# Moving eleven score-maximum slots of heads 1 to 3 in a fused attention and feed-forward kernel

## The chip, the cores and the metric

The kernel runs on one core of a Trainium2 chip. The metric is the device time of one execution in microseconds (us); shorter is better. The engines are called as the profile calls them: PE is TensorE (PEld its weight loads), DVE is VectorE, ACT is ScalarE, POOL is GpSimd, and SP is the engine whose queue issues nearly all DMAs.

## The reference

Attention over 4 batches x 8 heads, 768 positions, head dimension 64, in which a query sees only the keys with the same 6-bit hash; then a feed-forward layer of 512 x 2048 on the 3072 tokens.

```python
q_bits = (np.einsum('bhsd,dk->bhsk', q, proj) > 0)
k_bits = (np.einsum('bhsd,dk->bhsk', k, proj) > 0)
q_bucket = np.sum(q_bits * powers, axis=-1)
k_bucket = np.sum(k_bits * powers, axis=-1)
mask = q_bucket[:, :, :, None] == k_bucket[:, :, None, :]
scores = scale * np.matmul(q, k.transpose(0, 1, 3, 2))
scores = np.where(mask, scores, -1000000000.0)
scores = scores - np.max(scores, axis=-1, keepdims=True)
attn = np.exp(scores)
attn = attn / (np.sum(attn, axis=-1, keepdims=True) + 1e-09)
x = np.matmul(attn, v)
...
h = x @ w_in
g = np.where(h >= 1, h, np.where(h <= -1, 0.0, (h + 1) ** 2 / 4))
out = g @ w_out
```

## The kernel before

The 32 heads go in 16 pairs. A head is worked in 12 steps (NU): two halves (`hf`) of 384 query positions by six blocks (`j`) of 128 keys. One step of the loop over `g` holds three kinds of work.

**Scores and exponentials** (`s_unit`, L372 and L373). Two matmuls put a 128x384 block of scores into one of four `s` buffers of PSUM. The second one reads rows of `T2` that hold more than the query: rows 0 to 6 hold the hash bits, so that pairs with different hashes come out very negative, and row 7 (row 32 for heads 0 and 1) holds minus the row's maximum, so the subtraction of the maximum is part of the matmul. ACT then takes the exponential twice, once rounded (`ph`, L381) and once in full (L386), and the difference of the two becomes `pl` (`lo_unit`, L39): on DVE for four of the six key blocks, on POOL for two, one step later.

**Values** (`pv_unit`, L405, L407, L409). Three matmuls of the step four earlier (LAG) accumulate the output in one of two banks, `obank` (`o0`, `o1`). Ahead of the second and of the third one, the function `between` can insert something else.

**Maxima of a later head** (`max_mm`, L311, and `max_red`, L315). The row maxima must be there before a head's scores are. For each of its six query blocks a pair of matmuls writes 128x768 scores into the tile `smax`, of which there is only one, and DVE reduces them to one column of `nm`. Where the pairs stand is a table, `early`: slot 5g+2 lies in step g behind the scores and the subtraction, 5g+3 and 5g+4 ahead of the second and third value matmul, 5g+5 at the step's end. For 5g+2 to 5g+4 `max_red` is recorded right behind its pair. For 5g+5 it is held back and recorded in the next step behind the scores, so behind everything that the step's list of tasks has put on DVE's queue.

The program has a manual schedule: each engine's queue holds its instructions in the order in which the code records them, and waits only at its head.

**Tasks around the change.** The dictionary `tasks` gives each step things to do at its end. Those that matter:

- The hash bits of pair 1 (heads 2 and 3): in steps 8 and 10 `bits_mm` (four matmuls, L211, into an `obank`, and an ACT copy `neg`, L217); in steps 9 and 11 `bits_cmp` (DVE, L222); in step 11 `bits_scale` on ACT (L272, tile `bits`); in step 12 `bits_put`, four DMAs on SP (L283) into rows 0 to 7 of `T2`. The second DMA completes what head 2's maxima read.
- The same for pair 2 (heads 4 and 5) in steps 20, 21, 23 and 24: the second `bits_cmp` and `bits_scale` are tasks of step 24, and `bits_put` one of step 25.
- The maxima of head 2 go into row 7 in two halves: `half_clamp` (DVE) in steps 18 and 23, `half_put` in steps 19 and 25: a transpose on PE (L334), an ACT copy `te` (L336), and a DMA on SP (L338). For later heads it is `max_clamp`, `max_tr` (L350) and `max_put` (L357).
- SP's queue between: `bits_put`, moves of 384 KB between partitions (`move`, L164), the load of the values (`load_v`, L287, cast on ACT in L290), the stores of finished heads, then `half_put`.

Head 2's scores begin with step 24, head 3's with step 36. From slot 155 on, in step 30, the table is filled by another rule, with heads 4 to 31.

Of the kernel before, what the change touches and what calls it, by code (L numbers as in the profile page):

```python
# [25 lines left out]
NJ = S // P  # L26
# [88 lines left out]
def attention(ctx, tc, wst, T1, T2, qk, v, pj, cv, x_d, s_d, e_d, tasks, shared):  # L115
# [490 lines left out]
    NG = NH * NU  # L606
    red = None
    early = {}
    for hd, gs in ((0, (0, 2)), (1, (4, 5, 6, 8, 11, 12)), (2, (15, 16, 17, 19, 20, 22)), (3, (21, 23, 24, 26, 27, 29))):
        early.update({5 * n + 5: (hd, NJ - len(gs) + i) for i, n in enumerate(gs)})  # L610
    for i in range(2 * NJ):
        n = 5 * 31 + 35 * i // 4
        early[n + (n % 5 == 1)] = 4 + i // NJ, i % NJ
# [494 lines left out]
def lsh_attn_ffn(ctx: ExitStack, tc: tile.TileContext, qk, v, pj, cv, w_in, w_out, out):  # L1108
# [101 lines left out]
    for i in (2, 3):  # L1210
        at(NH * NU + 2 * i - 10, late[i + NFT - NW1][0])
    attention(actx, tc, wst, T1, T2, qk, v, pj, cv, x_d, s_d, e_d, tasks, attn)
    actx.close()

# [78 lines left out]
```

## Time and profile before

| what | value |
|---|---|
| median of three runs | 978.73 us (977.11 to 980.63) |
| the profiled execution's own time | 977.32 us |
| its span, first to last instruction | 975.5 us |
| granted TensorE clock | 0.999 |
| attention (maxima of heads run until) | about 439 us |
| HBM read, written | 106.13 MB, 33.87 MB |

In the rows of the profile stand the start in us from the span's start, the duration, the engine, the line, the operation and out<-in; in brackets the idle time of the engine ahead of the instruction, and what ended it. Matmuls are pipelined: one of 384 columns is shown with 0.34 us, though the next starts 0.175 us later. In the views of waits the numbers are the total in us, how often, and the longest.

### The profile page before, as it was taken

The page shows a single profiled execution, that of the slowest core. Times are in us where ns is not written, and L with a number is a line of the kernel's source. Part 1 is how long each engine was busy: PE and PEld are TensorE (multiplying, and loading weights), DVE is VectorE, ACT ScalarE, POOL GpSimd, SP SyncE. Part 2 cuts the span into 40 slices and gives each one's busy share as a digit, 9 for nine tenths or more (in the row PEclk, how much of TensorE's full clock was granted, in tenths as well). Part 3 has the DMA queues.
Part 4 walks back from the last instruction along what each step waited for, and adds up shares of the span by engine and source line. Part 5 has one row for each costly group of instructions (what it writes and reads, how often), then busy time and mean ns, then how long its engine had stood idle before and what let it go on. Part 6 is the DMA issues. An engine that isn't in the chain of part 4 may idle for free.

```text
span 975.5 us, 15546 instructions
## 1 busy us (share of the span) xinstructions
PE 962.4 (99%) x5050; PEld 890.8 (91%) x5050; DVE 788.5 (81%) x1355; ACT 680.3 (70%) x1481; POOL 354.9 (36%) x423
## 2 busy tenths in 40 slices
PE   8999999999999999999999999999999999999998
PEld 7899999999999999999989998888988888888896
DVE  8779999999999999896998797787876777655554
ACT  7889998999989998887656565455464545544444
POOL 8768887777788787566000000000000000000000
PEclk9999999999999999999999999999999999999999
DMA  5776666667766566545494579976458564454431
GB/s 161 187 189 172 162 165 166 175 184 200 180 178 176 150 171 175 147 110 141 136 330 154 152 227 301 296 231 200 119 169 231 147 182 117 149 152 119 119 87 65
DMA packets 95113, 167.56 MB, mean 172 GB/s; under 512 B 13956, under 2 KB 51960, under 8 KB 95032
## 3 DMA queue, kind: packets, MB, share of 16 engines
q1 hardware_dynamic: 94808, 166.56, 60.9%
q8 instruction: 40, 0.66, 0.3%
q14 instruction: 41, 0.34, 0.1%
q10 hardware_dynamic: 224, 0.00, 0.0%
HBM read 106.13 MB, written 33.87 MB: 144 GB/s over the span
## 4 chain that ended last, share of the span: by engine, by line
PE 87%; DVE 5%; POOL 5%; issue 1%; ACT 1%; DVEq 0%; POOLq 0%
PE y L831 27%; PE h L1063 18%; PE h L968 7%; PE smax L311 6%; PE s L373 5%; PE s L372 5%; PE o L407 5%; PE o L405 5%; PE o L409 5%; POOL t L39 3%; PE o L211 2%; DVE nm L315 2%; DVE pl L39 1%; POOL pl L39 1%; POOL t L153 1%
## 5 line engine op out<-in xcount | busy, mean ns | idle before, releaser
L381 ACT ACTIVATE ph<-s 128x384 fp32r<-128x384 f32 x380 | 188.7, 497 | 39.3 <-PE s L373 34.2
L315 DVE TENSOR_REDUCE nm<-smax 128x1 f32<-128x768 f32 x189 | 179.5, 950 | 20.4 <-PE smax L311 19.3
L39 POOL TENSOR_TENSOR pl<-pf,ph 128x384 fp32r<-128x384 f32 x128 | 134.2, 1052 | 77.8 <-ACT pf L386 77.8
L796 DVE SCALAR_TENSOR_TENSOR t<-t 128x384 f32<-128x384 f32 x128 | 71.3, 557 | 101.6 <-ACT z L791 101.3
L39 DVE TENSOR_TENSOR pl<-s,ph 128x384 fp32r<-128x384 f32 x256 | 135.5, 545 | 10.9 <-ACT s L386 9.2
L372 PE MATMUL s<-t 128*128 128x384 f32 x384 | 132.1, 344 | 0.0
L409 PE MATMUL o<-pl,va 128*128 128x386 f32 x384 | 130.4, 340 | 0.4 <-DVE pl L39 0.4
L407 PE MATMUL o<-ph,vb 128*128 128x386 f32 x384 | 130.1, 339 | 0.0
L405 PE MATMUL o<-ph,va 128*128 128x386 f32 x384 | 129.9, 338 | 0.0
L373 PE MATMUL s<-t 128*128 128x384 f32 x384 | 129.6, 337 | 0.0
L386 ACT ACTIVATE s<-s 128x384 f32<-128x384 f32 x252 | 125.5, 498 | 0.0
L831 PE MATMUL y<-t,ghi 128*128 128x512 f32 x384 | 124.7, 395 | 0.0
L311 PE MATMUL smax<-t 128*128 128x384 f32 x378 | 100.0, 346 | 4.3 <-DVE nm L315 4.2
L790 ACT ACTIVATE t<-h,mh 128x384 f32<-128x384 f32 x56 | 32.5, 581 | 84.4 <-PE h L968 44.4
L801 ACT CAST ghi<-z 128x384 fp32r<-128x384 f32 x129 | 65.2, 505 | 30.2 <-DVE z L797 26.4
L791 ACT ACTIVATE z<-t,m 128x384 f32<-128x384 f32 x128 | 79.0, 617 | 4.2
L831 PEld LDWEIGHTS y<-t,ghi 128*128 128x128 f32 x384 | 71.3, 188 | 11.1 <-ACT ghi L801 0.3
L1063 PE MATMUL h<-wbig,t 128*128 128x384 f32 x399 | 81.4, 336 | 0.0
L311 PEld LDWEIGHTS smax<-t 128*128 128x128 f32 x378 | 66.7, 188 | 14.2 <-DVE nm L315 13.5
L1063 PEld LDWEIGHTS h<-wbig,t 128*128 128x128 f32 x399 | 71.6, 188 | 5.3
L790 ACT ACTIVATE t<-wsq,mh 128x384 f32<-128x384 f32 x48 | 29.6, 617 | 67.0 <-DVE wsq L1076 40.7
L831 PE MATMUL y<-t,glo 128*128 128x512 f32 x192 | 76.0, 396 | 0.0
(190 smaller groups left out, 2144.3 us busy)
## 6 DMA issues: line engine op xcount, KB each, us to landing
t<-wc SPq DMA_DIRECT2D x92, 256.0 KB
t<-t SPq DMA_DIRECT2D x60, 384.0 KB
wraw<-wc SPq DMA_DIRECT2D x76, 256.0 KB
raw<-in_qk_dram SPq DMA_DIRECT2D x14, 768.0 KB
wraw<-in_w_in_dram SPq DMA_DIRECT2D x16, 512.0 KB
wraw<-in_w_out_dram SPq DMA_DIRECT2D x16, 512.0 KB
t<-ed SPq DMA_DIRECT2D x36, 192.0 KB
xd<-xs SPq DMA_DIRECT2D x32, 192.5 KB
```

The source lines that it names most:

```text
L39: eng.tensor_tensor(out=out, in0=a, in1=b, op=ALU.subtract)
L311: nc.tensor.matmul(out=smax[hd][:, hf, 0:HS], lhsT=t2[:, 0, h, i * P:(i + 1) * P], rhs=t2[:, 1, h, hf * HS:(hf + 1) * HS], start=True, sto ...
L315: nc.vector.tensor_reduce(out=nmp(hd)[:, i:i + 1], in_=smax[hd][:, :, 0:HS], axis=AX.XY, op=ALU.max, negate=True)
L372: nc.tensor.matmul(out=ps[:, 0:HS], lhsT=t1[:, 1, h, ks], rhs=t1[:, 0, h, sl], start=True, stop=False)
L373: nc.tensor.matmul(out=ps[:, 0:HS], lhsT=t2[:, 1, h, ks], rhs=t2[:, 0, h, sl], start=False, stop=True)
L381: nc.scalar.activation(out=ph[:, 0:HS], in_=ps[:, 0:HS], func=AF.Exp, scale=SCALE)
L386: nc.scalar.activation(out=pf, in_=ps[:, 0:HS], func=AF.Exp, scale=SCALE)
L405: nc.tensor.matmul(out=o, lhsT=wa, rhs=ph, start=(jj == 0), stop=False)
L407: nc.tensor.matmul(out=o, lhsT=wb, rhs=ph, start=False, stop=False)
L409: nc.tensor.matmul(out=o, lhsT=wa, rhs=pl, start=False, stop=(jj == NJ - 1))
L831: nc.tensor.matmul(out=ys[c][m], lhsT=g_[:, m * P:(m + 1) * P], rhs=w, start=(first and k == 0), stop=(last and k == 2))
L1063: nc.tensor.matmul(out=ps, lhsT=w[:, cs], rhs=x, start=(n == 0 and s not in (2, 3, 6)), stop=(n == 5), skip_group_check=True)
```

## The change

The table of slots for heads 0 to 3 is written as slot numbers instead of steps, and eleven of the slots are other ones.

```diff
-    for hd, gs in ((0, (0, 2)), (1, (4, 5, 6, 8, 11, 12)), (2, (15, 16, 17, 19, 20, 22)), (3, (21, 23, 24, 26, 27, 29))):
-        early.update({5 * n + 5: (hd, NJ - len(gs) + i) for i, n in enumerate(gs)})
+    for hd, gs in ((0, (5, 15)), (1, (25, 30, 37, 45, 57, 65)), (2, (80, 87, 93, 99, 105, 112)),
+                   (3, (118, 124, 130, 137, 143, 150))):
+        early.update({n: (hd, NJ - len(gs) + i) for i, n in enumerate(gs)})
```

| head | slots before | slots now |
|---|---|---|
| 0 | 5, 15 | 5, 15 |
| 1 | 25, 30, 35, 45, 60, 65 | 25, 30, 37, 45, 57, 65 |
| 2 | 80, 85, 90, 100, 105, 115 | 80, 87, 93, 99, 105, 112 |
| 3 | 110, 120, 125, 135, 140, 150 | 118, 124, 130, 137, 143, 150 |

Before, all of them lie at the end of a step, and head 3's first pair stands ahead of head 2's last. Now ten of them lie inside a step, in the order of the heads. ACT's, POOL's and SP's queues keep their order; PE's and DVE's change.

PE in steps 6 and 7, first before, then now. `smax` is the tile of the maxima, `s` of the scores, `o0` of the output; L311 x2 is the pair.

```order
L409 MATMUL o0_137<-pl_0_162,va_0_151 128x386
L311 MATMUL smax_415<-t2_0_77 128x384 x2
L372 MATMUL s_421<-t1_0_74 128x384
L373 MATMUL s_421<-t2_0_77 128x384
L405 MATMUL o0_137<-ph_4_159,va_0_151 128x386
```

```order
L409 MATMUL o0_137<-pl_0_162,va_0_151 128x386
L372 MATMUL s_418<-t1_0_74 128x384
L373 MATMUL s_418<-t2_0_77 128x384
L311 MATMUL smax_424<-t2_0_77 128x384 x2
L405 MATMUL o0_137<-ph_4_159,va_0_151 128x386
```

The pair of slot 35 went behind the two score matmuls of step 7, to slot 37.

DVE around step 11: L39 is the subtraction of step 10's block, L315 the reduction of slot 60 before and of slot 57 now, L222 the second bit comparison of pair 1. A piece of the difference:

```order
 L192 MEMSET t_0_77 1x768
 L39 TENSOR_TENSOR pl_165<-s,ph_158 128x384
-L222 TENSOR_TENSOR neg<-o_137,neg 32x384
-L315 TENSOR_REDUCE nm<-smax 128x1
+L315 TENSOR_REDUCE nm<-smax 128x1
+L222 TENSOR_TENSOR neg<-o_137,neg 32x384
 L39 TENSOR_TENSOR pl_166<-s,ph_159 128x384
 L315 TENSOR_REDUCE nm<-smax 128x1
```

The reduction went ahead of the comparison.

DVE from step 23 to step 28, first before, then now. `nm_692` and `nm_707` are head 3's maxima, `nmh` the clamped second half of head 2's, `pl_2` is the block of step 23, `pl_4` and `pl_5` those of steps 25 and 26, and L222 is the second bit comparison of pair 2.

```order
L315 TENSOR_REDUCE nm_692<-smax_711 128x1
L39 TENSOR_TENSOR pl_2_164<-s_701,ph_2_157 128x384
L222 TENSOR_TENSOR neg_666<-o0_137,neg_666 32x384
L315 TENSOR_REDUCE nm_692<-smax_733 128x1
L39 TENSOR_TENSOR pl_4_166<-s_741,ph_4_159 128x384
L315 TENSOR_REDUCE nm_692<-smax_770 128x1
L39 TENSOR_TENSOR pl_5_167<-s_761,ph_5_160 128x384
L315 TENSOR_REDUCE nm_692<-smax_789 128x1
```

```order
L39 TENSOR_TENSOR pl_2_164<-s_697,ph_2_157 128x384
L315 TENSOR_REDUCE nm_707<-smax_728 128x1
L222 TENSOR_TENSOR neg_666<-o0_137,neg_666 32x384
L315 TENSOR_REDUCE nm_707<-smax_747 128x1
L39 TENSOR_TENSOR pl_4_166<-s_738,ph_4_159 128x384
L39 TENSOR_TENSOR pl_5_167<-s_760,ph_5_160 128x384
L315 TENSOR_REDUCE nm_707<-smax_779 128x1
L315 TENSOR_REDUCE nm_707<-smax_798 128x1
```

Here too a reduction (slot 124) now stands ahead of the comparison, and the one of slot 137 stands behind the subtraction of step 26, where a reduction stood ahead of it.

## The prediction

> **What bounds the kernel now.** I read the page first, then the waits of the stretch that the change touches, then the rows of that stretch. From the page, the span, the busy time of TensorE (PE) and the chain that ended last:
>
> ```profile
> span 975.5 us, 15546 instructions
> PE 962.4 (99%) x5050; PEld 890.8 (91%) x5050; DVE 788.5 (81%) x1355; ACT 680.3 (70%) x1481; POOL 354.9 (36%) x423
> PE 87%; DVE 5%; POOL 5%; issue 1%; ACT 1%; DVEq 0%; POOLq 0%
> ```
>
> PE carries the end. The moved slots lie in steps 6 to 28 of 384, about 19 to 52 us. The view of waits between 14 and 60 us (us in total, times, longest) says what a better spacing could win there:
>
> ```profile
> PEld smax L311 <- DVE nm L315: 5.3, 10, 0.7
> PE smax L311 <- DVE nm L315: 2.1, 9, 0.4
> 14.36 0.30 PEld L311 LDWEIGHTS smax<-t 128*128 128x128 f32 x2 [0.67 <-DVE nm L315]
> 54.53 0.30 PEld L311 LDWEIGHTS smax<-t 128*128 128x128 f32 x2 [0.49 <-DVE nm L315]
> ```
>
> Ten maximum pairs find the one `smax` buffer still being reduced; the third and fourth line are two of them in the timeline (start, duration, in brackets the idle time ahead). What one costs, in step 12:
>
> ```profile
> 27.99 0.34 PE L409 MATMUL o<-pl,va 128*128 128x386 f32 x1
> 28.61 0.62 PE L311 MATMUL smax<-t 128*128 128x384 f32 x2 [0.28 <-DVE nm L315]
> 29.07 0.27 PE L350 MATMUL o<-ident,nm 128*12 128x128 f32 x1
> ```
>
> From the value matmul to what follows the pair are 1.08 us; unhindered it is three matmul pitches of 0.175 (0.18 between 31.69 and 31.87 below), 0.53. So 0.55 us is lost, close to the 0.60 that the weight load waits. All ten come to at most 5.3; 0.67 at 14.36 and 0.49 at 54.53 belong to pairs that the change leaves, so **4.1 us is the most that it can win**, 2.1 by PE's own row.
>
> **The change, part by part.** No instruction is added or removed: 11 pairs of score-maximum matmuls and their 11 reductions change places, at equal durations. What can move the time is who waits for whom.
>
> *Step 6 to 7, slot 35 to 37.* The pair now stands behind the two score matmuls of step 7 instead of ahead of them:
>
> ```profile
> 19.49 0.34 PE L409 MATMUL o<-pl,va 128*128 128x386 f32 x1
> 20.00 0.62 PE L311 MATMUL smax<-t 128*128 128x384 f32 x2 [0.17 <-DVE nm L315]
> 20.46 0.34 PE L372 MATMUL s<-t 128*128 128x384 f32 x1
> 21.01 0.49 ACT L381 ACTIVATE ph<-s 128x384 fp32r<-128x384 f32 x1 [0.33 <-PE s L373]
> 23.45 0.48 ACT L217 ACTIVATE neg<-o 32x384 f32<-32x384 f32 x1 [0.64 <-PE o L211]
> ```
>
> The scores fill 19.66 to 20.00, the pair starts at 20.00 as before, and PE is 0.35 us ahead afterwards. ScalarE (ACT), which idled 0.33 and 0.64 us for PE here, follows by 0.35.
>
> *Step 11, slot 60 to 57: a loss.* The pair goes into the middle of the step, so its reduction is issued on VectorE (DVE) ahead of the bit comparison (L222) of that step, which it followed before. Who waits for that comparison: ACT's `bits` (L272), behind it on ACT all later exponentials, and the DMAs that put the bits into the operands of heads 2 and 3.
>
> ```profile
> 26.11 0.49 ACT L386 ACTIVATE s<-s 128x384 f32<-128x384 f32 x1
> 26.68 0.56 DVE L39 TENSOR_TENSOR pl<-s,ph 128x384 fp32r<-128x384 f32 x1 [1.15 <-POOL nm L256]
> 27.16 0.54 DVE L222 TENSOR_TENSOR neg<-o,neg 32x384 f32<-32x384 f32 x1
> 27.51 0.49 ACT L386 ACTIVATE s<-s 128x384 f32<-128x384 f32 x1
> 27.62 0.94 DVE L315 TENSOR_REDUCE nm<-smax 128x1 f32<-128x768 f32 x1
> 27.92 1.01 ACT L272 ACTIVATE bits<-neg,cvt 32x768 fp32r<-32x768 f32 x1
> 29.00 2.94 SPq L283 DMA_DIRECT2D t<-bits  x4
> ```
>
> Before, the comparison ends at 27.70 and `bits` starts when ACT is free, 27.92. Now: the exponential 0.35 earlier at 25.76; the subtraction (L39) 0.57 behind it, 26.33; the reduction 0.48 later, 26.81, for 0.94; the comparison 27.75 to 28.29; `bits` at 28.3, **0.4 us later**, although ACT would be free at 27.6. If DVE's stages overlap by 0.1 it is 0.3, if ACT doesn't come earlier 0.7. Here a PE stall of 0.55 is traded for an ACT stall of 0.7. The release point of the bits is slot 80, the first pair of head 2:
>
> ```profile
> 31.69 0.34 PE L407 MATMUL o<-ph,vb 128*128 128x386 f32 x1
> 31.87 0.34 PE L409 MATMUL o<-pl,va 128*128 128x386 f32 x1
> 32.17 0.30 PEld L311 LDWEIGHTS smax<-t 128*128 128x128 f32 x2 [0.29 <-PE o L407]
> ```
>
> The weight load waits 0.29 us, and the engine named had not kept any earlier load waiting; the operand it reads is what the second of the four DMAs brings, issued at about 29.8 (a quarter of the 2.94 each). I take it that this is the wait. Then slot 80 goes to 32.17 + 0.4, and PE, which is 0.35 plus 0.5 us ahead by then, stands there. Its whole lead is gone and it is 0.4 us late.
>
> *Steps 16 to 24, slots 85 to 118.* Four or five pairs of the ten lie here. Suppose every wait of them goes, some 2 us: step 24 is then reached early, but its second score matmul reads row 7, the maxima of head 2's first half, which a DMA (L338) brings:
>
> ```profile
> 40.73 0.78 SPq L338 DMA_DIRECT2D t<-te  x1
> 45.96 0.34 PE L372 MATMUL s<-t 128*128 128x384 f32 x1
> 46.14 0.34 PE L373 MATMUL s<-t 128*128 128x384 f32 x1
> DMA packets 16, 0.10 MB, mean 197 GB/s; under 512 B 0, under 2 KB 0, under 8 KB 16
> DMA packets 25, 0.08 MB, mean 160 GB/s; under 512 B 12, under 2 KB 12, under 8 KB 25
> 57.68 0.92 SPq L357 DMA_DIRECT2D t<-te  x1
> 61.78 0.19 PEld L373 LDWEIGHTS s<-t 128*128 128x128 f32 x1 [0.18 <-DMA t<-te]
> ```
>
> The two rows of packets are 45.0 to 45.5 and 45.5 to 46.0 us. Packets under 512 B (the completions) come in the second half microsecond only, among the 6 KB pieces of the moves issued ahead of it. The like transfer for the next head (L357) takes 4.0 us from issue until PE may load. So the row lands between 44.8 (40.73 + 4.0) and 46.0; I take the late end, because of the twelve small packets. The SP queue that issues it is a chain behind `bits`: four DMAs, then moves that wait for one another. It shifts by the 0.4. **Step 24 can't pass its second score before about 46.4**; it is 0.3 us late whether the pairs before it wait or not.
>
> The Trainium skill, "DMA: Bandwidth & Descriptors", section "Anatomy of one DMA", gives about 2.0 us plus bytes over 436 GB/s for one transfer. By that the row would land at 42.8 and the wait would not be there; the measured 4.0 us behind two moves speaks against it.
>
> *Step 24, slot 120 to 124: the larger loss.* Again the reduction of the moved slot passes ahead of a comparison, the one of pair 2.
>
> ```profile
> 46.80 0.54 DVE L222 TENSOR_TENSOR neg<-o,neg 32x384 f32<-32x384 f32 x1
> 47.43 1.02 ACT L272 ACTIVATE bits<-neg,cvt 32x768 fp32r<-32x768 f32 x1
> 48.35 0.46 ACT L381 ACTIVATE ph<-s 128x384 fp32r<-128x384 f32 x1
> 49.66 0.46 ACT L386 ACTIVATE s<-s 128x384 f32<-128x384 f32 x1
> 49.76 0.95 DVE L315 TENSOR_REDUCE nm<-smax 128x1 f32<-128x768 f32 x1
> 50.76 0.62 PE L311 MATMUL smax<-t 128*128 128x384 f32 x2 [0.31 <-DVE nm L315]
> 52.09 0.34 PE L372 MATMUL s<-t 128*128 128x384 f32 x1
> ```
>
> Now: second score 46.45; two value matmuls, pair at 46.98; reduction 0.52 behind it (a pitch and one matmul's 0.34), 47.5, for 0.94; comparison to 49.0; `bits` at 49.05 instead of 47.43, **1.6 us late**, and ACT's queue with it: the second exponential of step 26 goes from 49.66 to 51.25. Its subtraction follows by 0.57, 51.8, and DVE issues the reduction of slot 137 only behind it (before, the reduction at this place stood ahead of it): 52.3 to 53.25. Slot 143 in step 28 needs that buffer: pair at 53.3, next matmul 0.46 behind as at 28.61, two value matmuls, step 29 at 54.1 against 52.09. **PE is 2.0 us late**; the stall of 50.76 is gone, but one of 1.5 stands in step 28.
>
> *Behind step 30* the order is the old one, and PE has little to give back: 2.0 us of such waits in five places between 60 and 440 us, which move along, since what they wait for is late too. The 0.18 at 61.78 can be saved. I take +1.9; if ACT or DVE overlap more than I count it is 1.0, with the 0.7 of step 11 it is 2.6.
>
> ```profile
> PE smax L311 <- DVE nm L315: 2.0, 5, 0.5
> ```
>
> Sum: 977.3 + 1.9 = 979.2 us for the profiled execution's own time. That one lies 1.4 under the median of three runs, 978.7 (977.1 to 980.6); I go half-way, so everything below stands 0.7 higher: **979.9**.
>
> **The rivals.**
> *All waits go* (4.1 less some 0.4 left over): 977.3 - 3.7 + 0.7 = 974.3. For it: DVE is only 81% busy. Against it: both `bits` and the row of step 24. 6%.
>
> *The rows land early.* If L338's row takes 2.4 us, as the second bit DMA does from 29.8 to 32.17, it is there at 43.5 even 0.4 late; nothing holds step 24, and PE keeps up to 1.2 of the 2 us. The second `bits` is then 0.4 late instead of 1.6, and step 29 some 0.8: 978.8. The page of the Trainium skill weighed above would have it so. Against it: the 4.0 us at 57.68 and the small packets. 18%.
>
> *Clearly slower: the bits of pair 2 hold slot 155 in step 30.* They are issued behind the row of head 2's second half, which waits for ACT: at 52.2 us by my count, and with 3.2 us as at 29.00 there at 55.4; PE comes at 54.53 + 2.0 = 56.5. The margin is 1.1. If the four DMAs stand behind the value load and a move and take 5.3, as L338's row does at 40.73, it is overrun by 1.0, and the next moves slip too; I price it at 1.5: 977.3 + 1.9 + 1.5 + 0.7 = 981.4. It decides once they take over 4.3 us. 13%.
>
> **How the numbers follow.** The forecast has 63%, own range 979.0 to 980.6. A measurement of this kernel tells about 0.3% (2.9 us) from no change. Faster by more: the first rival, 0.05. Slower by more than 2.9: the last one and the upper end of the forecast, 0.22. Within: 0.73. The range goes from 977.0 (the second rival, 978.8, less the 1.6 by which the fastest run lies under the median, and a little of the first) to 982.6 (the forecast's upper end plus the 1.9 of the slowest run, which takes in most of the last).
>
> **What would show it.** Right: `bits` (L272) starts at about 28.3 and 49, with ACT idle for DVE's L222 ahead of it (0.7 and 1.4 us); the weight load of slot 80 near 32.5; a score load of step 24 waiting over 1 us for the DMA; one PE wait over 1 us for L315 near 53 us; behind 60 us the same rows, about 1.9 later. Wrong: no ACT wait at L272; step 24 reached well before 46 us without a wait; or the shift at 60 us given back before 440.

## The result and the profile after

| what | before | after |
|---|---|---|
| median of 22 runs each, side by side | 979.53 us (977.11 to 981.07) | 980.59 us (979.04 to 981.94) |
| ratio | | 1.0015, 95% interval 1.0009 to 1.0021 |
| the profiled execution's own time | 977.32 us | 979.68 us |
| its span | 975.5 us | 977.9 us |

The changed kernel is 0.15% slower: within the 0.3% that the prediction counts as no change, with the whole interval on the slower side. The forecast was 979.9, 1.2 above the recorded median of before; measured is 1.06 above the median of before beside it, and that median lies 0.80 higher than the recorded one. Here and below, the ratio and its interval are those on record; the ratio is not the quotient of the two medians.

From the page of the changed kernel, span, busy time and chain, to be laid beside the three lines of before:

```profile
span 977.9 us, 15542 instructions
PE 961.8 (98%) x5050; PEld 890.1 (91%) x5050; DVE 788.5 (81%) x1355; ACT 679.8 (70%) x1481; POOL 354.7 (36%) x423
PE 86%; POOL 5%; DVE 5%; DMA 2%; ACT 1%; issue 1%; DVEq 0%; POOLq 0%
```

The work is the same to 0.1%, and the span has grown by 2.4 us. New in the chain that ended last is DMA, with 2%. The view of waits from 14 to 60 us says what came in (us in total, times, longest):

```profile
PEld smax L311 <- DVE nm L315: 4.2, 8, 1.6
POOL t L153 <- DMA raw<-in_qk_dram: 2.9, 1, 2.9
ACT bits L272 <- DVE neg L222: 1.9, 2, 1.3
PE smax L311 <- DVE nm L315: 1.8, 3, 1.3
PE smax L311 <- DMA t<-bits: 1.0, 1, 1.0
```

Before, PE's own waits for the reduction (fourth line) were nine of at most 0.4 us; now they are three, one of them of 1.3. The spread did remove short waits, and a long one took their place. The third line is the wait that the prediction is built on; the second is one that it does not contain.

The timeline of the changed kernel through the moved slots, all engines, in order of time:

```profile
20.12 0.61 PE L311 MATMUL smax<-t 128*128 128x384 f32 x2
26.45 0.56 DVE L39 TENSOR_TENSOR pl<-s,ph 128x384 fp32r<-128x384 f32 x1 [0.91 <-POOL nm L256]
26.93 0.96 DVE L315 TENSOR_REDUCE nm<-smax 128x1 f32<-128x768 f32 x1
27.80 0.54 DVE L222 TENSOR_TENSOR neg<-o,neg 32x384 f32<-32x384 f32 x1
28.37 1.03 ACT L272 ACTIVATE bits<-neg,cvt 32x768 fp32r<-32x768 f32 x1 [0.61 <-DVE neg L222]
32.66 0.59 PE L311 MATMUL smax<-t 128*128 128x384 f32 x2 [1.03 <-DMA t<-bits]
41.80 1.12 SPq L338 DMA_DIRECT2D t<-te  x1
45.79 0.44 PE L373 MATMUL s<-t 128*128 128x384 f32 x1 [0.30 <-DMA t<-te]
46.97 0.96 DVE L315 TENSOR_REDUCE nm<-smax 128x1 f32<-128x768 f32 x1 [0.20 <-PE smax L311]
47.84 0.54 DVE L222 TENSOR_TENSOR neg<-o,neg 32x384 f32<-32x384 f32 x1
48.41 1.03 ACT L272 ACTIVATE bits<-neg,cvt 32x768 fp32r<-32x768 f32 x1 [1.27 <-DVE neg L222]
51.64 0.95 DVE L315 TENSOR_REDUCE nm<-smax 128x1 f32<-128x768 f32 x1
52.64 0.62 PE L311 MATMUL smax<-t 128*128 128x384 f32 x2 [1.29 <-DVE nm L315]
56.44 0.33 PE L372 MATMUL s<-t 128*128 128x384 f32 x1
```

Twice a reduction (L315) now runs just ahead of the bit comparison (L222), and twice ACT idles for that comparison ahead of `bits` (0.61 and 1.27 us), where before it did not wait. The first delay ends at slot 80 (32.66, released by the DMA of the bits), the second at slot 143 (52.64). The last row is step 31, where the order of both kernels is the same again. It starts at 56.44; before, it started here:

```profile
54.99 0.33 PE L372 MATMUL s<-t 128*128 128x384 f32 x1
```

So 1.45 us of the 2.4 arise in the moved slots. The rest arises at step 36, in these rows of the changed kernel's timeline:

```profile
51.87 0.50 POOL L153 CAST t<-raw 128x384 fp32r<-128x384 f32 x1 [2.86 <-DMA raw<-in_qk_dram]
58.51 1.15 SPq L164 DMA_DIRECT2D t<-t  x2
59.76 1.21 SPq L357 DMA_DIRECT2D t<-te  x1
64.17 0.44 PE L373 MATMUL s<-t 128*128 128x384 f32 x1 [0.79 <-DMA t<-te]
```

and of the kernel before (the rows of L357 and of PE's load for step 36, 57.68 and 61.78, stand in the prediction):

```profile
49.51 0.51 POOL L153 CAST t<-raw 128x384 fp32r<-128x384 f32 x1
56.14 1.16 SPq L164 DMA_DIRECT2D t<-t  x2
```

The raw load of pair 3 (L148) arrives too late for POOL's first cast, which starts 2.36 us later than in the trace of before. Of this, 0.80 is that the load is issued later (44.06 against 43.26 in the timelines); the rest is that it takes longer. POOL's casts and subtractions of that pair slip, the moves of their results (L164) with them, the row of maxima (L357) is queued behind these on SP, and the second score matmul of step 36 waits for it. From there to the end the shift stays at 2.4.

### The profile page after: what moved, and what is told of

Read it like the earlier page. It is cut to its first block, busy times and chain, and to the rows that moved or that the text cites. A ratio compares the mean times of both kernels' runs of the same rounds, so it can differ in the third digit from the quotient of the medians.

```text
span 977.9 us, 15542 instructions
## 1 busy us (share of the span) xinstructions
PE 961.8 (98%) x5050; PEld 890.1 (91%) x5050; DVE 788.5 (81%) x1355; ACT 679.8 (70%) x1481; POOL 354.7 (36%) x423
## 4 chain that ended last, share of the span: by engine, by line
PE 86%; POOL 5%; DVE 5%; DMA 2%; ACT 1%; issue 1%; DVEq 0%; POOLq 0%
PE y L832 27%; PE h L1064 18%; PE h L969 7%; PE smax L311 6%; PE s L373 5%; PE s L372 5%; PE o L407 5%; PE o L405 5%; PE o L409 5%; POOL t L39 3%; PE o L211 2%; DVE nm L315 1%; DVE pl L39 1%; POOL pl L39 1%; DMA t<-te 1%
## 5 line engine op out<-in xcount | busy, mean ns | idle before, releaser
L315 DVE TENSOR_REDUCE nm<-smax 128x1 f32<-128x768 f32 x189 | 179.4, 949 | 20.7 <-PE smax L311 19.8
L39 POOL TENSOR_TENSOR pl<-pf,ph 128x384 fp32r<-128x384 f32 x128 | 134.1, 1052 | 77.7 <-ACT pf L386 77.7
L39 DVE TENSOR_TENSOR pl<-s,ph 128x384 fp32r<-128x384 f32 x256 | 135.5, 545 | 12.7 <-ACT s L386 10.0
L372 PE MATMUL s<-t 128*128 128x384 f32 x384 | 132.0, 344 | 0.0
L311 PE MATMUL smax<-t 128*128 128x384 f32 x378 | 100.0, 345 | 5.2 <-DVE nm L315 3.8
L791 ACT ACTIVATE t<-h,mh 128x384 f32<-128x384 f32 x56 | 32.5, 581 | 84.2 <-PE h L969 44.4
L311 PEld LDWEIGHTS smax<-t 128*128 128x128 f32 x378 | 66.7, 188 | 14.7 <-DVE nm L315 12.4
```

What stands on the lines that cost most here:

```text
L39: eng.tensor_tensor(out=out, in0=a, in1=b, op=ALU.subtract)
L311: nc.tensor.matmul(out=smax[hd][:, hf, 0:HS], lhsT=t2[:, 0, h, i * P:(i + 1) * P], rhs=t2[:, 1, h, hf * HS:(hf + 1) * HS], start=True, sto ...
L315: nc.vector.tensor_reduce(out=nmp(hd)[:, i:i + 1], in_=smax[hd][:, :, 0:HS], axis=AX.XY, op=ALU.max, negate=True)
L372: nc.tensor.matmul(out=ps[:, 0:HS], lhsT=t1[:, 1, h, ks], rhs=t1[:, 0, h, sl], start=True, stop=False)
```

## The experiments

Three questions were open. Are the two reductions that passed ahead of a bit comparison the cause of the 1.45 us? What is the late load, and does the change bring it? And can the part that the prediction counted as a gain be had alone? In the first table are times; in the second, where step 31 and step 37 start (L372 in the timeline of the run's one profile), and how long POOL's first cast of pair 3 waits (in e1 and e8 the view puts that wait down to another DMA). PE's very first score matmul starts between 11.94 and 12.30 us in these profiles, after waits for the first loads, so differences up to 0.3 us at step 31 can come from there.

| run | median of its runs | before beside it | ratio, interval |
|---|---|---|---|
| e1_hoist | 979.52 (12) | 979.78 | 1.0006, 0.9995 to 1.0017 |
| e2_undo57 | 980.09 (11) | 979.78 | 1.0007, 0.9998 to 1.0016 |
| e3_undo124 | 980.29 (11) | 979.78 | 1.0012, 1.0003 to 1.0021 |
| e4_undo_both | 980.20 (12) | 979.78 | 1.0009, 0.9999 to 1.0019 |
| e6_before_split | 978.43 (11) | 979.40 | 0.9991, 0.9982 to 1.0001 |
| e7_after_split | 979.60 (11) | 979.40 | 0.9998, 0.9989 to 1.0007 |
| e8_hoist_split | 978.78 (12) | 979.40 | 0.9993, 0.9984 to 1.0002 |
| e9_split_37 | 977.66 (12) | 979.11 | 0.9985, 0.9976 to 0.9994 |
| e10_split_again | 978.50 (12) | 979.11 | 0.9996, 0.9986 to 1.0006 |
| e11_split_37_again | 977.77 (12) | 980.38 | 0.9977, 0.9968 to 0.9986 |
| e12_only_37 | 978.66 (12) | 980.38 | 0.9989, 0.9978 to 1.0000 |

| profile | step 31 | step 37 | POOL's wait for the raw load |
|---|---|---|---|
| before | 54.99 | 62.95 | none |
| before, another execution (e5) | 56.00 | 65.84 | 3.13 |
| after | 56.44 | 65.33 | 2.86 |
| e1_hoist | 55.54 | 65.34 | 3.06 |
| e2_undo57 | 56.10 | 64.98 | 2.85 |
| e3_undo124 | 57.43 | 66.72 | 3.75 |
| e4_undo_both | 56.25 | 65.25 | 3.45 |
| e6_before_split | 55.20 | 63.04 | none |
| e7_after_split | 56.55 | 64.38 | 1.76 |
| e8_hoist_split | 55.39 | 64.30 | 2.16 |
| e9_split_37 | 54.70 | 62.97 | 0.53 |
| e10_split_again | 55.01 | 63.00 | none |
| e11_split_37_again | 54.72 | 62.66 | none |
| e12_only_37 | 54.90 | 62.73 | none |

### e1: the comparisons ahead of the reductions

The new slots are kept, and both second comparisons are recorded ahead of the reductions that had passed them.

```diff
-    at(11, bits_cmp, 1, 1)
...
-                at(g + n + 1, bits_cmp, pr + 2, hf)
+                if g + n + 1 != 24:
+                    at(g + n + 1, bits_cmp, pr + 2, hf)
...
+        if g in (11, 24):
+            bits_cmp(1 if g == 11 else 2, 1)
```

> All slots as in the changed kernel; only the second bit comparison of pairs 1 and 2 is recorded ahead of the reductions of slots 57 and 124 instead of behind them. Queue theory (the loss comes from the reduction that passed ahead of the comparison): L272 starts without waiting for L222, at about 27.8 and 47.2 us instead of 28.4 and 48.4; the PE wait of 1.3 us ahead of slot 143 is at most 0.4; the time is 1.5 to 3 us under the changed kernel, so 0 to 1.5 us under the kernel before. Rival 1 (pairs inside a step cost by themselves, whatever DVE's order): stays about 1.5 us over the kernel before. Rival 2 (only the DMAs in line set it): the score of step 24 and of step 36 still wait for te, and the time stays within 0.4 us of the changed kernel.

```profile
27.89 1.01 ACT L272 ACTIVATE bits<-neg,cvt 32x768 fp32r<-32x768 f32 x1
47.37 1.03 ACT L272 ACTIVATE bits<-neg,cvt 32x768 fp32r<-32x768 f32 x1 [0.43 <-DVE neg L222]
64.18 0.44 PE L373 MATMUL s<-t 128*128 128x384 f32 x1 [1.24 <-DMA t<-te]
```

In its timeline both `bits` are back at the times of before (27.92 and 47.43), the second still with 0.43 us of ACT's idle time, the long wait of slot 143 is gone, and step 31 starts 0.9 us earlier than in the changed kernel. But step 36 waits 1.24 us for the row `te`, and step 37 starts at 65.34, as in the changed kernel: the gain is swallowed there. The ratio went from the changed kernel's 1.0015 to 1.0006, which can't be told from before. The 1.5 to 3 us that the queue theory expected did not come: the median is 1.07 under the changed kernel's.

### e2, e3, e4: one reduction, the other, both put back

```diff
-(1, (25, 30, 37, 45, 57, 65))
+(1, (25, 30, 37, 45, 60, 65))
```

```diff
-(3, (118, 124, 130, 137, 143, 150))
+(3, (118, 125, 130, 137, 143, 150))
```

e2 has the first edit, e3 the second, e4 both. In e3 slot 124 goes to 125 and not to the 120 of before; what it restores is the order, since the reduction of slot 125 is recorded behind the comparison.

> The changed kernel with slot 57 put back to 60. Queue theory: the first L272 is back at about 27.7 us and slot 80 starts without the 1.0 us wait for bits, but the second L272 still waits for L222 and slot 143 still stalls by more than 1 us; the time is 0.3 to 0.8 us under the changed kernel, about 0.7 to 1.2 over the kernel before. Rival 1: as the changed kernel less a tenth of a microsecond. Rival 2: step 24 reaches its second score as late as in the changed kernel, no gain.

> The changed kernel with slot 124 put back to 125. Queue theory: the first L272 is still at 28.4 us and slot 80 still waits, but the second L272 starts without waiting for L222, the stall ahead of slot 143 is under 0.5 us, and the time is 1 to 1.6 us under the changed kernel, within 0.5 us of the kernel before. Rival 1: as the changed kernel. Rival 2: as the changed kernel.

> The changed kernel with 57 put back to 60 and 124 to 125; the other nine moved slots stay. Queue theory: both L272 start without a wait for L222; the time is 0 to 1.5 us under the kernel before. Rival 1 (pairs inside steps): over the kernel before by about 1.2 us, since eight pairs still lie inside steps. Rival 2: as the changed kernel.

The timeline of e2, then of e3, ACT's two `bits` and PE's long wait:

```profile
27.80 1.01 ACT L272 ACTIVATE bits<-neg,cvt 32x768 fp32r<-32x768 f32 x1
48.08 1.03 ACT L272 ACTIVATE bits<-neg,cvt 32x768 fp32r<-32x768 f32 x1 [1.28 <-DVE neg L222]
52.31 0.61 PE L311 MATMUL smax<-t 128*128 128x384 f32 x2 [1.29 <-DVE nm L315]
```

```profile
28.72 1.03 ACT L272 ACTIVATE bits<-neg,cvt 32x768 fp32r<-32x768 f32 x1 [0.78 <-DVE neg L222]
33.01 0.59 PE L311 MATMUL smax<-t 128*128 128x384 f32 x2 [1.03 <-DMA t<-bits]
47.92 1.03 ACT L272 ACTIVATE bits<-neg,cvt 32x768 fp32r<-32x768 f32 x1 [0.31 <-DVE neg L222]
56.26 0.44 PE L373 MATMUL s<-t 128*128 128x384 f32 x1 [1.49 <-DMA t<-te]
```

Each edit takes away its own pair of waits and leaves the other: without slot 57, ACT's first wait and slot 80's stall are gone; without slot 124, the 1.28 of the second `bits` falls to 0.31 and slot 143 no longer stalls. That settles the mechanism. The time does not follow: all three kernels, and the changed one, stay within their intervals of each other. Of the queue theory's times only e2's came (0.50 under the changed kernel's median); e3 is 0.30 under it instead of 1 to 1.6, and e4 is 0.42 over the kernel before instead of at or under it. Nor is e4 the 1.2 over that rival 1 expected: with eight pairs still inside steps its step 28 starts at 50.42, 0.80 before that of the first profile (up to 0.34 of it from an earlier first matmul), and a wait in step 30 takes this lead away. In e3 and e4 another wait stands in the same place, the second score of step 30 for the second half of head 2's row (1.49 here, 1.38 in e4), and all three have POOL waiting 2.85 to 3.75 us for the raw load, and step 36 for `te`.

### e5: the kernel before, once more

> The kernel before, unchanged: a second look at its execution. Raw theory (since the first four runs): what the lead of one variant over another in steps 24 to 30 is worth is taken away in step 36, because the last sixteenth of one load of raw data lands 1.5 us behind the others, POOL's casts start late, and the row te for step 36 stands in SP's queue behind the moves of that data; the recorded execution of the kernel before, in which POOL didn't wait, would then be one of its quick ones. Expected by it: POOL waits 1.5 to 3.5 us for raw at about 50 us, the score of step 36 waits over 0.8 us for te, span about 977 to 978. Rival (the recorded one is typical): POOL's cast starts at 49.5 without a wait for the DMA, step 36 waits 0.2, span 975.5 within 0.7.

One execution, 980.27 us. From its timeline:

```profile
52.39 0.50 POOL L153 CAST t<-raw 128x384 fp32r<-128x384 f32 x1 [3.13 <-DMA raw<-in_qk_dram]
54.84 0.45 PE L373 MATMUL s<-t 128*128 128x384 f32 x1 [0.92 <-DMA t<-te]
64.68 0.44 PE L373 MATMUL s<-t 128*128 128x384 f32 x1 [1.25 <-DMA t<-te]
65.84 0.34 PE L372 MATMUL s<-t 128*128 128x384 f32 x1
```

The late load is not the change's doing: the unchanged kernel has it in this execution (8.6 us from issue to first cast, 7.8 in the changed kernel's, at most 6.25 in the first profile), waits at step 30 and at step 36, and starts step 37 at 65.84, later than the changed kernel (65.33). The profile from which the prediction was made shows an execution without it, which is 1.4 to 3.1 us under the medians of before (978.73 to 980.38 in six comparisons); of the 22 runs beside the changed kernel six lie as low as it (977.11 to 977.72), the other sixteen from 978.7 up.

### e6, e7, e8: the raw load in two halves

The load of pair 3 is issued in two halves, so that POOL's first two casts need only the first; applied to the kernel before, to the changed one and to e1.

```diff
-        for sl in (slice(0, HS), slice(HS, S)) if pr == 1 else (slice(0, S),):
+        for sl in (slice(0, HS), slice(HS, S)) if pr in (1, 3) else (slice(0, S),):
```

> The kernel before, with the load of raw data for heads 6 and 7 in two DMAs of half the columns each, as it is for heads 2 and 3 already; POOL's first two casts and subtractions read only the first. Raw theory: POOL starts by 49 us in any execution, step 36 waits at most 0.3 us for te, time 0.5 to 2 us under the kernel before. Rival: same within 0.4 us, or slower by up to 0.5 because SP issues one DMA more.

> The changed kernel with the same load in two. Raw theory: the stalls of slots 80 and 143 stay, but POOL starts by 49.5 and step 36 waits at most 0.3 us for te; 0.8 to 1.5 us under the changed kernel, and the difference to the kernel before with the split load grows to about 1.5 to 2 us, as forecast for the queue on ACT. Rival (queue theory alone): within 0.4 us of the changed kernel.

> The changed kernel with both bit comparisons ahead of the reductions and the load in two. Raw theory with the queue theory: no L272 wait over 0.5 us, no stall over 0.5 us in step 28, step 36 waits at most 0.3 us; 1 to 2.5 us under the kernel before, and under the changed kernel with the split load by 1.5 to 2. Rival (queue theory alone): as with the comparisons ahead and one load, 0 to 0.6 us from the kernel before.

In none of the three profiles does step 37 start later than 64.4 (with whole loads that arrived late: 65.0 to 66.7). Step 37 in e6, then in e7:

```profile
63.04 0.34 PE L372 MATMUL s<-t 128*128 128x384 f32 x1
```

```profile
48.54 1.03 ACT L272 ACTIVATE bits<-neg,cvt 32x768 fp32r<-32x768 f32 x1 [1.49 <-DVE neg L222]
52.76 0.62 PE L311 MATMUL smax<-t 128*128 128x384 f32 x2 [1.29 <-DVE nm L315]
64.38 0.34 PE L372 MATMUL s<-t 128*128 128x384 f32 x1
```

Neither waits for `te` at step 36, so these two profiles show the change's price without the late row: 1.34 us at step 37. The medians differ by 1.17 (979.60 and 978.43), the fastest runs by 1.32 (978.63 and 977.31), and seven of e6's eleven runs are quicker than the quickest of e7. With the comparisons hoisted as well (e8) the median is 978.78, 0.82 under e7's and 0.35 over e6's: most of the price goes with the order of reduction and comparison. Its one profile doesn't show that gain (step 37 at 64.30): POOL waits 2.16 us there, and step 36 0.81 for `te`. The sizes expected came in part: e6 is 0.97 under the kernel before, but its interval touches 1; e7 is 1.17 over e6, not 1.5 to 2; e8 is 0.62 under the kernel before, not 1 to 2.5, and 0.82 under e7, not 1.5 to 2.

### e9 to e12: the gaining move alone

Of the eleven moves only slot 35 to 37 is made, with the load in two halves (e9, e11) and whole (e12); e10 is e6 again.

```diff
-        early.update({5 * n + 5: (hd, NJ - len(gs) + i) for i, n in enumerate(gs)})
+        early.update({5 * n + 5 + 2 * (n == 6): (hd, NJ - len(gs) + i) for i, n in enumerate(gs)})
```

> The kernel before with the raw load of pair 3 in two halves, and of the eleven moves only the one that the prediction counted as a gain: slot 35 to 37. Step 7's first score should stand about 0.35 us earlier than in the split kernel before. Theory A (the gates behind it set the time: the bits at slot 80 and the row of step 24 come no earlier, so a lead is lost there): the profile shows the lead at step 7, a longer wait of slot 80's weight load for the DMA of the bits than before's 0.29, and nothing of it at step 24; the time is the split kernel's, 978.4, within 0.3. Rival B (the lead reaches step 31, since the bits follow it: ACT and DVE are ahead as well): step 31 starts near 54.8 where the split kernel has 55.2, and the time is 978.0 to 978.1. Rival C (the move costs something that the two larger losses had covered): above 978.9.

> The kernel before with the raw load of pair 3 in two halves, once more on another chip, since its first interval, 0.9982 to 1.0001, ended at no change. Theory A (the late end of that load costs the kernel before about 1 us in most of its executions, and two halves let the first casts start on time): ratio 0.999, time 0.9 to 1.0 us under the kernel before, and the profile shows no wait of POOL's first cast of pair 3 (L153) over 0.5 us and no wait over 0.5 us of step 36's second score for te. Rival B (the first result was a chip's chance, the quick executions of before being as many as the split kernel's): ratio 1.000, and the wait at L153 is there again with about 3 us.

> Slot 35 to 37 with the raw load of pair 3 in two halves, once more on another chip. In the first run its median was 0.84 us under the split kernel beside it, but the one profile showed no lead at step 31 beyond that of the program's start. Theory A (the two edits together end the late executions): ratio 0.9985 again, median 977.5 to 978.2, highest run under 979. Rival B (the first run's twelve executions were a lucky draw): ratio 0.9991 to 0.9996, as the split kernel alone, and single runs near 980.

> The kernel before with slot 35 to 37 alone, the load whole. Theory A (the split is what starts POOL's casts on time, slot 37 gives no lead that lasts): the time is that of the kernel before, within 0.4 us, and single runs reach 980 to 981 as its own do. Rival B (slot 37 alone keeps the executions quick): median 0.8 us or more under the kernel before, at 978.6 or less, with no run over 979.5.

Both edits together are faster than the kernel before in both comparisons, by 0.15% and 0.23%, with intervals clear of 1, though under the 0.3% bound. It is the best version found. Each edit alone ends at or beside 1. e10's profile has no wait at L153 (its theory A), but its ratio, 0.9996, is closer to rival B's, so the split alone is worth 0.04 to 0.09% and not shown to be a gain. e11 came out as its theory A in the median, not in its highest run (979.51). e12 fits neither of its theories: 1.7 us under the median beside it, with an interval that touches 1 and single runs up to 981.05.

The profile of e9 shows why a lead does not simply last. POOL's first cast, and step 36:

```profile
49.52 0.50 POOL L153 CAST t<-raw 128x384 fp32r<-128x384 f32 x1 [0.53 <-DMA raw<-in_qk_dram]
61.81 0.44 PE L373 MATMUL s<-t 128*128 128x384 f32 x1 [0.17 <-DMA t<-te]
```

Slot 80's weight load no longer waits (31.73, and 32.22 with a wait of 0.29 in e10), step 31 starts at 54.70 against e10's 55.01; but POOL now idles 0.53 us for the load, and step 37 starts at 62.97 against 63.00. Of the lead at step 31, 0.26 can come from the first score matmul, which starts at 12.01 against 12.27. So this profile's lead ends at the row of step 36, not at slot 80 or step 24, where theory A put its end, while the medians went with rival B and beyond.

e11's profile shows the other case. Its first score matmul starts at 12.30, as e10's, step 31 at 54.72, and POOL does not wait: step 37 starts at 62.66, so there 0.34 of lead gets past the row of step 36. The fastest runs agree: e9's and e11's are 0.33 and 0.81 us under the fastest of before beside them. That the rest of their gain lies in fewer late executions fits their narrow runs (highest 978.57 and 979.51), but no profile of theirs fell in one with a late row: why slot 37 should help there is open.

## Why the prediction was right, and where not

**The direction, the two losses and the verdict: right.** The two places where a reduction goes ahead of the comparison were named with their consequences, and each was confirmed by undoing it (e2, e3). Step by step, forecast against the changed kernel's trace:

| step of the prediction | forecast | measured |
|---|---|---|
| pair of slot 37 starts at | 20.00 | 20.12 |
| first `bits`, ACT idle | 28.3, 0.7 | 28.37, 0.61 |
| weight load of slot 80 | 32.5 | 32.63 |
| second score of step 24 not before | 46.4 | 45.79 |
| weight load of that score waits for the DMA | over 1 | 0.62 |
| second `bits`, ACT idle | 49.05, 1.4 | 48.41, 1.27 |
| slot 143's pair | 53.3 | 52.64 |
| lateness of PE behind it | 2.0 | 1.45 |

*Slot 80's release* was inferred from an operand: the view named a PE instruction, the prediction took the DMA of the bits. Now the view itself names that DMA (32.66, 1.03 us), and in e2, where `bits` is on time, the wait is gone.

*The gate of step 24* is the term that was mis-sized, by 0.6 us; everything behind it came 0.6 early, and slot 143 with it, which makes 1.45 out of 2.0. The gate itself is there: PE has up to 0.6 us of idle time for `te`. Two choices went wrong against each other. I took the late end, 46.0, for the landing of the row in the kernel before, because of the small packets; and I let its issue slip by 0.4. The issue slipped by 1.07 (40.73 to 41.80), and the transfer took 3.94. Of the 1.07, 0.46 stand already at the issue ahead of it (L358, 40.06 to 40.52), as forecast; the other 0.61 is that this issue held the queue longer (last section). The chain of work of the changed kernel has it:

```profile
41.80 3.94 DMA t<-te
59.76 4.37 DMA t<-te
```

That is the 4.0 of the like row at 57.68 (4.1 by the two rows shown), the early end of the two that the prediction had. A time measured on the same kind of transfer was better than a reading of packet sizes. The Trainium skill's 2.0 us plus bytes ("DMA: Bandwidth & Descriptors", section "Anatomy of one DMA"), which the prediction set against it, is stated there for DMAs issued from GpSimd, while these two are issued by SP; it is not what they show: 3.94 us for 1.5 KB and 4.37 for 3 KB, with 384 KB moves issued ahead of them. (40.73 plus 2.0 is 42.7, where the prediction has 42.8; nothing hangs on it.)

*The sum* ended near the measurement in part by luck, for a reason that it did not contain. Its "+1.9 against the profiled execution" became +2.36 in the profile: 1.45 by the mechanism forecast, some 0.9 by the load that came late. "I go half-way" to the median (0.7) stood in for something that was not looked for: what the executions above 977.3 do differently. Those that were profiled of these two kernels wait for the raw load, then for `te` at step 36 (another loss, of 0.9 us, is in the last section). In these two executions the unchanged kernel starts step 37 at 65.84 and the changed one at 65.33, so the slots hardly matter there, as far as one execution of each can tell; in e6 and e7, without the wait, they cost 1.34. The medians differ by 1.06, which lies between, and the fastest runs by 1.93 (977.11 and 979.04): none of the 22 runs of the changed kernel was as quick as the six of before.

*The shift carried to the end* held: from step 37 to step 383, the last, the changed kernel stays 2.4 behind (458.10 against 455.70 at L372), and PE's five waits for L315 between 60 and 440 us are unchanged.

**The rivals.** "All waits go" fell: PE's short waits for the reduction went, and the gates of slot 80, step 24 and slot 143 took them back. "The rows land early" had the wait too short: step 24 does wait, and slot 143 does stall. "Clearly slower", the bits of pair 2 at slot 155, did not happen: the pair of step 30 waits 0.16 us, for DVE. The place that came in instead, POOL's raw load and step 36, was among none of them. In the prediction it is one clause: "the 0.18 at 61.78 can be saved". Those 0.18 us were the sign that step 36 stands right at its gate, and that any slip on the queues behind that row would be paid in full.

**Open.** Why the raw load ends late in six of the eight profiled executions that load it whole. Of the 16 completions that the changed kernel's trace records for it, 15 come by 50.12 us and the last at 51.72; in the quick execution of before all sixteen come between 48.43 and 49.36. The other five late executions have it too: the last completion comes 1.4 to 1.8 us behind the fifteenth. One instruction fetch (0.02 MB) falls between 44 and 52 us in both, which alone explains nothing. Two edits that would settle more, the load issued earlier and L357 issued ahead of the moves, weren't tried.

## What to carry to other kernels

When a step is moved into the middle of another engine's program, look on every in-order queue for what it now stands ahead of: here a reduction that nobody was waiting for delayed a short comparison on which another engine and a chain of DMAs hung, which cost more than the stalls that the better spacing removed. A wait of a few tenths for a DMA on the critical engine marks a gate: price what arrives late there, not only what may be saved. And where the runs of a kernel spread by several times the effect, find out first which wait separates its quick executions from the others, since a single profile shows only one of the two.

## What was not expected of the hardware

One 768 KB load, with the same instructions around it, let the first cast start at 49.5 us in one execution of the same kernel and at 52.39 in another (3.13 us of waiting); that execution starts step 37 2.89 us later, most of the spread of 977.1 to 981.1 us.

A second place makes executions differ, and it lies outside the stretch that the change touches. In step 370 a subtraction on POOL and a multiplication on DVE (L711) start within 0.04 us of each other. In ten of the fourteen profiles DVE's takes 0.55 us and POOL's 1.43 to 1.45; in e1, e2, e8 and e11 POOL's takes 1.02 and DVE's 1.39 or 1.40, PE then waits for DVE's `pl`, and the last steps come 0.9 us later. First before, then e11:

```profile
441.40 1.44 POOL L39 TENSOR_TENSOR pl<-pf,ph 128x384 fp32r<-128x384 f32 x1 [0.81 <-ACT pf L386]
441.42 0.55 DVE L711 TENSOR_TENSOR raw<-raw,t 128x384 f32<-128x384 f32 x1
```

```profile
441.27 1.02 POOL L39 TENSOR_TENSOR pl<-pf,ph 128x384 fp32r<-128x384 f32 x1 [0.80 <-ACT pf L386]
441.31 1.39 DVE L711 TENSOR_TENSOR raw<-raw,t 128x384 f32<-128x384 f32 x1
444.59 0.45 PE L409 MATMUL o<-pl,va 128*128 128x386 f32 x1 [0.44 <-DVE pl L39]
```

So the profiled times of e1 (980.74), e2 (980.34), e8 (979.67) and e11 (978.02) hold 0.9 us that no edit of slots, comparisons or the load explains. How often it falls in the other runs is not known, and neither is what decides which of the two instructions is the long one.

And a DMA's issue on SP's queue is no constant: the one just ahead of the row of step 24 (L358) took 0.57 us before and 1.18 after, which is more than half of that row's slip of 1.07. It isn't the change's doing: in e5, the kernel before again, it took 1.15.

```profile
40.06 0.57 SPq L358 DMA_DIRECT2D ed<-te  x1
```

```profile
40.52 1.18 SPq L358 DMA_DIRECT2D ed<-te  x1
```
